# Transposing k and q of six chunks in 64x64 tiles of the TensorE array, one PSUM bank for each chunk

## The chip, the cores and the metric

The kernel runs on one core of one Trainium2 chip. The metric is the device time of one execution in microseconds (us); lower is better. "The span" is the time from the first to the last instruction in the profile of one execution; the device time holds the span and a little around it.

## What is computed

A sliding-window causal attention feeds a gated feed-forward block. Cut to what matters:

```
scores = q @ k.T / sqrt(64)           # 8 batches, 8 heads, 576 positions, head size 64
mask   = 0 <= (query - key) < 64      # each query sees itself and the 63 keys before it
x      = softmax(scores, mask) @ v    # -> [4608 tokens, 512]
out    = (silu(x @ w_gate) * (x @ w_val)) @ w_out     # 512 -> 1536 -> 512
```

Inputs and the output are float32 in memory; on the chip nearly all operands are bfloat16, with sums in float32 in PSUM.

## The kernel before

The 4608 tokens are cut into 36 chunks of 128 tokens for the attention, and into 9 tiles of 512 tokens (four chunks) for the feed-forward block. One list of operations is written out by hand in the function build (L1020). A small planner (class _Graph) keeps the order in which the operations stand in that list for each engine, and puts in a semaphore wait wherever an operation reads what another engine wrote, or overwrites what another engine still reads. So every engine works strictly through its own list, and an operation that has to wait holds up all that stand behind it on its engine.

**The attention of a chunk** needs kT and qT, that is k and q with the head dimension along the partitions. Loads bring k and q in with tokens along the partitions. There are three ways to turn them round:
- Chunks 0 to 3 go through first_T and first_ev (L816, L833) at the start.
- Chunks 10 to 35 go through the function T (L360), a transposing DMA on SyncE's queue.
- Chunks 4 to 9 are turned by TensorE, a pair of chunks (256 tokens) at a time. These three pairs are what the change touches. Pair 4/5 and pair 8/9 go through T2 (L371, TensorE work at L382). Pair 6/7 goes through first_T(..., 1) (L816, TensorE work at L825) and first_ev (L833), because its loads lie in another layout.

In T2 a partition of the source holds two neighbouring tokens, so 128 partitions hold the 256 tokens of the pair. For one of k and q it issues 16 transposes. Each takes 128 partitions x 64 columns (one head, one of the two tokens) as the loaded operand, streams a 128x128 identity past it, and writes 64 partitions x 128 columns of PSUM. The two heads of a couple (index p) go to the lower and the upper 64 PSUM partitions, so two such transposes stand side by side in the array. All 16 fill one PSUM bank with both chunks of the pair. ScalarE (called ACT in the profile) then copies the bank to kT or qT, as one copy of 128x1024 elements, or as two of 128x512 where the ring of chunk slots wraps (q of pair 8/9) or in first_ev (one for each chunk). All copies are made at L260. k and q are separate operations in separate banks.

**The scores** of two chunks are made by S2 (L735): for each chunk Sb (L450) issues 24 small matmuls on 64x64 tiles (L464 and L468), and ACT takes the exponential (L476, two operations for each chunk). The scores of a chunk need kT of the chunk before and of itself, and its own qT. **The weighted sum over v** follows in AV2 (L741, TensorE work at L582), which issues 64 matmuls of 64x64 tiles for two chunks; later pairs go through B2 and AVpair (L692).

**The feed-forward block** F(c, (f,)) (L896) makes 128 of the 1536 hidden columns for 512 tokens: four matmuls with Wg (L888), a tanh on ACT (L869), four matmuls with Wv (L888), and two operations on VectorE (DVE; L874, L876). O (L910) is the second matrix product (12 matmuls at L930), with its copy out and its store. X (L762) turns a finished attention chunk round for the feed-forward block: four TensorE transposes (L784) and a copy (L260).

**PSUM banks.** There are eight. The function bank (L225) gives the bank that was last touched by the oldest operation in the list, except those in the set held; pair (L235) gives two neighbouring banks, and two (L492) two banks that both stay in held until they are taken out.

The order around the three pairs, as it stands in build:

```
F(0,(6,))  T2(2,"k") T2(2,"q")            F(0,(7,))  S2(4)  F(0,(8,)) F(0,(9,)) AV2(4) F(0,(10,))
first_T k, first_T q, first_ev k6, k7     X(4)  F(0,(11,)) with X(5) inside  first_ev q6, q7  F(1,(0,1),0,256)  S2(6) ...
F(1,(5,))  T2(4,"k") T2(4,"q")            F(1,(6,))  S2(8)  F(1,(7,)) ...
```

The loads are issued by GpSimd (POOL): those of pair 4/5 in early_loads (L984, load2 at L332), those of pair 6/7 in more_loads (L992, next_load at L803), followed there by Wo (load_wo, L347), and those of pair 8/9 in late_loads (L1000).

Of the kernel before, what the change touches and what calls it, by code (L numbers as in the profile page):

```python
# [7 lines left out]
B, H, S, D = 8, 8, 576, 64  # L8
DM, DFF = H * D, 1536
T = B * S  # L10
# [7 lines left out]
BF = dt.bfloat16  # L18
# [135 lines left out]
class _Kernel:  # L154
# [213 lines left out]
        self.g.op("sp", lambda e: e.dma_start_transpose(d, src[:, :]), reads=[(x + "n", i, j) for j in range(2)],  # L368
                  writes=[(x + "T", z, 0), (x + "T", z, 1)], dma=True)

    def T2(self, st, x):  # L371
        src = (self.ks2 if x == "k" else self.qs2)[st % 2]
        dst = self.kT if x == "k" else self.qT
        nz = self.NZ if x == "k" else self.ZQ
        bank, bk = self.bank("a")
        tb = bank.bitcast(BF).rearrange("p (c j t) -> p c j t", c=4, j=2)

        def pe(e):
            for c in range(4):
                for j in range(2):  # L380
                    for p in range(2):
                        r = e.transpose(tb[64 * p:64 * p + 64, c, j, :], src[:, 2 * c + p, j, :], self.ident[:, :])  # L382
            return r

        self.g.op("pe", pe, reads=["ident", ("s2", x, st % 2, 0), ("s2", x, st % 2, 1)], writes=[bk])
        a = tb.rearrange("p c j t -> p c t j")

        def ev(eng, lo=0, hi=2):
            z0 = (2 * st + lo) % nz
            if z0 + hi - lo > nz:  # L390
                ev(eng, 0, 1)
                ev(eng, 1, 2)
                return
            d = dst[:, :, 128 * z0:128 * (z0 + hi - lo)].rearrange("p c (t j) -> p c t j", j=2)
            self.copy(eng, d, a[:, :, 64 * lo:64 * hi, :], [bk], [(x + "T", z, b) for z in range(z0, z0 + hi - lo) for b in range(2)])

        return ev

    def var(self, n):
        b0 = (2 * n) % BPB == 0  # L400
        b1 = (2 * n + 1) % BPB == 0
        return 1 if b0 else (2 if b1 else 0)
# [359 lines left out]
    def X(self, n, eng="sp", kind="f"):  # L762
        if n >= NCH:
            return
        g = self.g
        ix, it, u = n % 4, (n // 4) % self.NX, n % 4
        xb = self.xb[ix]
        xo = self.xT[it][:, :, 128 * u:128 * u + 128]
        xk = [("xb", ix, 0), ("xb", ix, 1)]
        if eng == "sp":  # L770
            g.op("sp", lambda e: e.dma_start_transpose(xo, xb[:, :]), reads=xk, writes=[("xT", it, u)], dma=True)
            return
        self.Xp(n, kind)(eng)
# [122 lines left out]
    def F(self, c, fs, lo=0, hi=512, mid=None, side=False):  # L896
        do = self.Fp(c, fs, lo, hi, side)
        for a in range(len(fs)):
            do("Wg", a)
        if mid:  # L900
            mid()
        do("tan", 0)
        for a in range(len(fs)):
            do("Wv", a)
        do("end", 0)
# [112 lines left out]
        self.T(n, "q")  # L1018

    def build(self):  # L1020
        F, S, AV, X, T2, O = self.F, self.S, self.AV, self.X, self.T2, self.O
        self.loads()
        self.banks("a", [4, 5, 6, 7, 0, 1, 2, 3, 4, 5, 0, 1, 2, 3, 4, 5, 6, 7, 0, 1, 2, 3, 4, 5, 6, 7, 6, 7])
        self.lru = True
# [3 lines left out]
        fk = self.first_T("k")  # L1028
        self.first_ev("k", 0, "dve", fk)
        fq = self.first_T("q")  # L1030
# [6 lines left out]
        fk = self.first_T("k", 1)  # L1037
# [3 lines left out]
        s2 = self.Sa(2, True)  # L1041
        fq = self.first_T("q", 1)
# [40 lines left out]
        F(0, (4,))  # L1083
        F(0, (5,))
        F(0, (6,))
        T2(2, "k")("act")
        T2(2, "q")("act")
        self.late_loads()
        F(0, (7,))
        self.S2(4)  # L1090
# [1 line left out]
        F(0, (9,), side=True)  # L1092
        self.AV2(4)
        F(0, (10,))
        fk = self.first_T("k", 1)
        self.held.add(fk[1][1])
        fq = self.first_T("q", 1)
        self.held.add(fq[1][1])
        self.first_ev("k", 6, "act", fk)
        self.first_ev("k", 7, "act", fk)  # L1100
        self.held.discard(fk[1][1])
        X(4, "act")
        F(0, (11,), mid=lambda: X(5, "act"))
        self.first_ev("q", 6, "act", fq)
        self.first_ev("q", 7, "act", fq)
        self.held.discard(fq[1][1])
        F(1, (0, 1), 0, 256)
        self.S2(6)
        F(1, (2, 3), 0, 256)
# [10 lines left out]
        F(1, (4,))  # L1120
        self.init_kmask()
        F(1, (5,))
        T2(4, "k")("act")
        T2(4, "q")("act")
        for n in (10, 11):
            self.load(n, "v", self.lastF)
        for n in (12, 13):
# [31 lines left out]
        for c in range(2, NFC):  # L1159
            for u in range(4):  # L1160
                n = 4 * c + u + 4
# [6 lines left out]
                v = u + 1 if c == 2 else u  # L1168
# [71 lines left out]
```

## Time and profile before

| what | value |
|---|---|
| device time, median of 3 runs | 326.89 us (326.6 to 327.25) |
| span of the profiled execution | 324.8 us |
| that execution's own device time | not listed apart from the runs; the median is 2.1 us above the span |
| mean granted TensorE clock | 1.000 |
| VectorE busy | 215.8 us (66%) |
| ACT busy | 125.8 us (39%) |
| GpSimd busy | 104.2 us (32%) |

The page of the profile lists busy times, a strip of 40 slices, the chain of work that ended last, and groups of instructions with the same line and shape. "PE" is TensorE's matmuls and "PEld" its operand loads, which run beside them. Views of the trace used below: the chain in order of time (start, length, what), the timeline (start, length, engine, line, operation, tiles, count, and in brackets the idle time before it with what ended it), groups by line and shape (count, busy us, mean ns of one, idle time), windows (start:end, length, then busy time and number of instructions that touch the window, granted clock, DMA share, GB/s), the list of waits (us in total, times, longest) and DMA issues (count, KB each, us from issue to landing). Times in these views count from the start of the span. A matmul's listed length holds its way through the array; the next one starts long before it ends, so TensorE's pace is read from starts.

### The profile page before, as it was taken

The numbers are of one execution on the slowest core, as the hardware profiler recorded it, in microseconds if no ns is written. First come the engines' busy times: TensorE is split into PE (matmuls) and PEld (weight loads), VectorE is DVE, ScalarE is ACT, GpSimd is POOL, SyncE is SP. The second block draws the span as 40 slices with busy tenths as digits, with TensorE's granted clock in tenths as the row PEclk, the third lists the DMA queues.
The fourth block names the chain that finished last, engine by engine and source line by source line (L and its number), as shares of the span: only waits on it lengthen the run. The fifth ranks groups of instructions, "written<-read, shape, count | busy, mean of one in ns | idle before, by whom it ended". The sixth has DMA issues, their size and how long they took to land.

```text
span 324.8 us, 7717 instructions
## 1 busy us (share of the span) xinstructions
PE 319.2 (98%) x3278; PEld 162.4 (50%) x3278; DVE 215.8 (66%) x400; ACT 125.8 (39%) x224; POOL 104.2 (32%) x134
## 2 busy tenths in 40 slices
PE   6999999999999999999999999999999999999996
PEld 5665565564544454545454444545454544444444
DVE  5886866688485966676768585958576767555510
ACT  3935563634332443333333242424242422222311
POOL 6999831142626061607060607060402000000000
DMA  7999999999999899959998998999687202000012
GB/s 189 179 191 186 205 172 167 161 150 149 158 138 167 128 100 137 163 109 152 119 115 122 146 141 81 146 132 163 71 110 96 69 32 67 32 34 32 32 67 97
DMA packets 154354, 39.83 MB, mean 123 GB/s; under 512 B 140368, under 2 KB 149328, under 8 KB 154320
## 3 DMA queue, kind: packets, MB, share of 16 engines
q0 software_dynamic: 104896, 18.36, 72.8%
q1 hardware_dynamic: 43952, 11.15, 24.7%
q10 hardware_dynamic: 5472, 9.83, 9.5%
q8 instruction: 26, 0.43, 0.5%
q14 instruction: 8, 0.07, 0.1%
HBM read 37.75 MB, written 9.44 MB: 145 GB/s over the span
## 4 chain that ended last, share of the span: by engine, by line
PE 96%; DMA 1%; ACT 1%; DVE 0%; SPq 0%; issue 0%
PE ps L888 58%; PE ps L930 29%; PE ps L692 2%; PE ps L514 2%; DMA hT<-in_q_dram 1%; PE ps L464 1%; PE ps L825 1%; ACT pt L447 1%; PE ps L382 1%; PE ps L420 1%; PE ps L582 1%; PE ps L468 0%; DVE ost L261 0%; PE ps L784 0%; PE ps L439 0%; ACT xT L260 0%
## 5 line engine op out<-in xcount | busy, mean ns | idle before, releaser
L874 DVE SCALAR_TENSOR_TENSOR uu<-sig,ps 128x512 bf16<-128x512 bf16 x108 | 73.9, 685 | 57.3 <-ACT sig L869 57.1
L888 PE MATMUL ps<-xT,Wg 128*128 128x512 bf16 (+1 forms) x456 | 111.2, 369 | 0.1
L888 PE MATMUL ps<-xT,Wv 128*128 128x512 bf16 (+1 forms) x456 | 111.0, 368 | 0.0
L869 ACT ACTIVATE sig<-ps 128x512 bf16<-128x512 f32 x108 | 65.1, 603 | 89.0 <-PE ps L888 89.0
L930 PE MATMUL ps<-Wo,hT 128*128 128x512 bf16 (+1 forms) x444 | 98.8, 374 | 0.0
L876 DVE SCALAR_TENSOR_TENSOR hT<-uu,ps 128x512 bf16<-128x512 bf16 x108 | 74.2, 687 | 3.7
L888 PEld LDWEIGHTS ps<-xT,Wv 128*128 128x128 bf16 x456 | 44.5, 98 | 48.4
L930 PEld LDWEIGHTS ps<-Wo,hT 128*128 128x128 bf16 x444 | 43.3, 98 | 49.2
L888 PEld LDWEIGHTS ps<-xT,Wg 128*128 128x128 bf16 x456 | 42.7, 98 | 45.5 <-ACT xT L260 0.6
L330 POOL DMA_DIRECT2D kn<-in_k_dram x29 | 24.9, 861 | 107.7 <-PE ps L888 103.7
L330 POOL DMA_DIRECT2D va<-in_v_dram x40 | 34.4, 889 | 34.0 <-PE ps L888 34.0
L260 ACT ACTIVATE ost<-ps 128x512 f32<-128x512 f32 (+1 forms) x22 | 12.9, 587 | 52.9 <-PE ps L930 52.9
L261 DVE COPY ost<-ps 128x512 f32<-128x512 f32 (+1 forms) x15 | 10.1, 674 | 30.1 <-PE ps L930 30.1
L524 ACT ACTIVATE pt<-ps 128x512 bf16<-128x512 f32 x36 | 18.6, 603 | 29.0 <-PE ps L514 29.0
L330 POOL DMA_DIRECT2D qn<-in_q_dram x29 | 25.1, 870 | 0.3 <-issue 0.3
L476 ACT ACTIVATE pt<-ps 128x512 bf16<-128x512 f32 x28 | 14.5, 603 | 12.9 <-PE ps L468 12.9
L727 DVE TENSOR_TENSOR xb<-ps,rc 128x512 bf16<-128x512 f32 (+2 forms) x39 | 18.8, 510 | 0.5
L692 PE MATMUL ps<-va,pt 64*64 64x65 bf16 x800 | 12.3, 192 | 0.0
L490 DVE TENSOR_TENSOR pt<-pt,kmask 128x1024 bf16<-128x1024 bf16 x18 | 11.5, 683 | 0.0
L692 PEld LDWEIGHTS ps<-va,pt 64*64 64x64 bf16 x800 | 10.3, 107 | 0.0
L723 DVE RECIPROCAL rc<-ps 128x8 f32<-128x8 f32 (+2 forms) x39 | 5.7, 174 | 6.5 <-PE ps L692 6.5
L490 DVE TENSOR_TENSOR pt<-pt,mask 128x1024 bf16<-128x1024 bf16 x14 | 9.3, 686 | 0.9 <-ACT pt L476 0.8
(76 smaller groups left out, 131.6 us busy)
## 6 DMA issues: line engine op xcount, KB each, us to landing
out_dram<-ost ACTq DMA_DIRECT2D x35, 256.0 KB, 2.9
va<-in_v_dram POOLq DMA_DIRECT2D x32, 128.0 KB, 5.5
kn<-in_k_dram POOLq DMA_DIRECT2D x23, 128.0 KB, 4.2
qn<-in_q_dram POOLq DMA_DIRECT2D x23, 128.0 KB, 4.5
Wg<-in_moe_w_gate_dram POOLq DMA_DIRECT2D x6, 256.0 KB, 6.6
Wv<-in_moe_w_val_dram POOLq DMA_DIRECT2D x6, 256.0 KB, 7.4
Wo<-in_moe_w_out_dram POOLq DMA_DIRECT2D x2, 768.0 KB, 15.3
ks<-in_k_dram POOLq DMA_DIRECT2D x2, 256.0 KB, 7.1
```

What stands on the lines that cost most here:

```text
L260: return self.g.op("act", lambda e: e.activation(d, a, ACTF.Copy), reads=reads, writes=writes, after=after)
L330: self.g.op("pool", lambda e, d=d, a=a: e.dma_start(d, a), writes=ks, dma=True, after=gate)
L476: g.op("act", lambda e, po=po, p=p: e.activation(po, sv[p], ACTF.Exp, scale=SCALE), reads=[bx[p][1]], writes=[pk[p]])
L490: self.g.op("dve", lambda e: e.tensor_tensor(pt, pt, m, ALU.mult), reads=pk + mk, writes=pk)
L524: g.op("act", lambda e, po=po, p=p: e.activation(po, sv[p], ACTF.Exp, scale=SCALE), reads=[bx[p][1]], writes=[pk[p]])
L692: x = e.matmul(o, ab[0], ab[1], start=first, stop=phase == 1, skip_group_check=True)
L727: g.op("dve", lambda e, av=av, hs=hs, w=w, rc=rc, xo=xo: e.tensor_tensor(xo[:, :, hs, :], av[:, :, :, 0:64], rc[:, :, hs].unsqueeze(3).to_ ...
L869: g.op("act", lambda e: e.activation(sig[:, 0:w], G[:, 0:w], ACTF.Tanh, scale=0.5), reads=[gk], writes=[("sig", i)])
L874: g.op("dve", lambda e: e.scalar_tensor_tensor(uu[:, 0:w], sig[:, 0:w], 1.0, G[:, 0:w], ALU.add, ALU.mult), reads=[("sig", i), gk], writes ...
L876: g.op("dve", lambda e: e.scalar_tensor_tensor(out, v3(uu), 0.5, v3(V), ALU.mult, ALU.mult), reads=[("uu", i), vk], writes=[("hT", ih, f) ...
L888: r = e.matmul(bank[:, a * n:a * n + n], W[:, kk, f * 128:f * 128 + 128], xT[:, kk, lo:hi], start=(kk == 0), stop=(kk == NK - 1))
L930: r = e.matmul(OB[:, 0:n], hT[:, f, 128 * u:128 * u + 128], self.Wo[:, f, lo:hi], start=(f == 0), stop=(f == NF - 1))
```

## The change

T2 goes, and one function T64 turns k and q of a pair in one TensorE operation. Each transpose now takes 64 partitions x 64 columns as the loaded operand, streams 64 columns of the identity, and writes 64 partitions x 64 columns. The index u (chunk of the pair, partitions 64u to 64u+63 of the source) picks the PSUM bank, and p the half of the PSUM partitions. A bank then holds k (first half) and q (second half) of one chunk. There are 64 transposes for a pair where there were 32 (16 for k, 16 for q). The two banks are taken by two(), each held until both copies of its chunk stand in the list. The copies are four for each pair, 128x512 each: in Tkq2 (pairs 4/5 and 8/9) in the order k, q of the first chunk, k, q of the second; for pair 6/7 the first chunk's two before X(4) and the second's two after F(0,(11,)), where k of both chunks stood before and q of both after. For pairs 4/5 and 8/9 a copy now reads PSUM in a row and writes every second element of kT or qT; before, it read PSUM with a step and wrote in a row. Loads, scores and everything else stay as they are.

```diff
-    def T2(self, st, x):
...
-            for c in range(4):
-                for j in range(2):
-                    for p in range(2):
-                        r = e.transpose(tb[64 * p:64 * p + 64, c, j, :], src[:, 2 * c + p, j, :], self.ident[:, :])
...
+    def T64(self, st):
+        n = 2 * st
+        bx = self.two()
+        loads = []
...
         def pe(e):
+            for i, (x, src, _) in enumerate(loads):
+                for a in range(8):
+                    for u in range(2):
+                        r = slice(64 * u, 64 * u + 64)
+                        for p in range(2):
+                            o = bx[u][0].bitcast(BF)[64 * p:64 * p + 64, 512 * i + 64 * a:512 * i + 64 * a + 64]
+                            y = src[r, a, p, :] if st == 3 else src[r, 2 * (a // 2) + p, a % 2, :]
+                            z = e.transpose(o, y, self.ident[r, r])
+            return z
+
+        rd = ["ident"] + [k for _, _, ks in loads for k in ks]
+        self.g.op("pe", pe, reads=rd, writes=[b[1] for b in bx])
+
+        def ev(x, u, eng):
+            bank, bk = bx[u]
...
+            if st == 3:
+                a, d = a.rearrange("p (j g c) -> p c g j", j=8, c=4), d.rearrange("p c (g j) -> p c g j", j=8)
+            else:
+                a, d = a.rearrange("p (c j t) -> p c j t", c=4, j=2), d.rearrange("p c (t j) -> p c j t", j=2)
+            self.copy(eng, d, a, [bk], [(x + "T", z, 0), (x + "T", z, 1)])
+            left.discard((x, u))
+            if not any(v == u for _, v in left):
+                self.held.discard(bk[1])
...
+    def Tkq2(self, st):
+        ev = self.T64(st)
+        for u in range(2):
+            for x in "kq":
+                ev(x, u, "act")
...
-        T2(2, "k")("act")
-        T2(2, "q")("act")
+        self.Tkq2(2)
...
-        fk = self.first_T("k", 1)
-        self.held.add(fk[1][1])
-        fq = self.first_T("q", 1)
-        self.held.add(fq[1][1])
-        self.first_ev("k", 6, "act", fk)
-        self.first_ev("k", 7, "act", fk)
-        self.held.discard(fk[1][1])
+        ev = self.T64(3)
+        ev("k", 0, "act")
+        ev("q", 0, "act")
         X(4, "act")
         F(0, (11,), mid=lambda: X(5, "act"))
-        self.first_ev("q", 6, "act", fq)
-        self.first_ev("q", 7, "act", fq)
-        self.held.discard(fq[1][1])
+        ev("k", 1, "act")
+        ev("q", 1, "act")
...
-        T2(4, "k")("act")
-        T2(4, "q")("act")
+        self.Tkq2(4)
```

More of the change, by code (lines that the diff above doesn't have):

```diff
@@ L369, in T @@
                   writes=[(x + "T", z, 0), (x + "T", z, 1)], dma=True)
-    def T2(self, st, x):
[L372 to L376, printed above, removed]
-        def pe(e):
-            for c in range(4):
-                for j in range(2):
-                    for p in range(2):
[L382 to L395, printed above, removed]
-        return ev
@@ new lines, in T64 @@
+    def T64(self, st):
[4 more added lines that the diff above has]
+            if st == 3:
+                loads.append((x, *self.first[x, 1]))
+            else:
+                loads.append((x, (self.ks2 if x == "k" else self.qs2)[st % 2], [("s2", x, st % 2, i) for i in range(2)]))
+        def pe(e):
+            for i, (x, src, _) in enumerate(loads):
[11 more added lines that the diff above has]
+            bank, bk = bx[u]
+            i = "kq".index(x)
+            a = bank.bitcast(BF)[:, 512 * i:512 * i + 512]
+            z = (n + u) % (self.NZ if x == "k" else self.ZQ)
+            d = (self.kT if x == "k" else self.qT)[:, :, 128 * z:128 * z + 128]
+            if st == 3:
+                a, d = a.rearrange("p (j g c) -> p c g j", j=8, c=4), d.rearrange("p c (g j) -> p c g j", j=8)
+            else:
+                a, d = a.rearrange("p (c j t) -> p c t j", c=4, j=2), d.rearrange("p c (t j) -> p c t j", j=2)
+            self.copy(eng, d, a, [bk], [(x + "T", z, 0), (x + "T", z, 1)])
+            left.discard((x, u))
+            if not any(v == u for _, v in left):
+                self.held.discard(bk[1])
+        left = {(x, u) for x in "kq" for u in range(2)}
+        return ev
@@ L399, in var @@
+    def Tkq2(self, st):
+        ev = self.T64(st)
+        for u in range(2):
+            for x in "kq":
+                ev(x, u, "act")
     def var(self, n):
@@ L1020, in build @@
     def build(self):
-        F, S, AV, X, T2, O = self.F, self.S, self.AV, self.X, self.T2, self.O
+        F, S, AV, X, O = self.F, self.S, self.AV, self.X, self.O
         self.loads()
```

## The prediction

> **What bounds the kernel now.** I read the page first: how busy each engine is, and which chain ended last.
>
> ```profile
> span 324.8 us, 7717 instructions
> PE 319.2 (98%) x3278; PEld 162.4 (50%) x3278; DVE 215.8 (66%) x400; ACT 125.8 (39%) x224; POOL 104.2 (32%) x134
> PE 96%; DMA 1%; ACT 1%; DVE 0%; SPq 0%; issue 0%
> ```
>
> TensorE is busy for 98% of the span and makes up 96% of the chain. So time taken off TensorE shortens the run, unless a wait appears where it was. Next the chain in order of time: the three pairs stand on it as TensorE work.
>
> ```profile
> 28.16 1.01 PE ps L382 x32
> ...
> 37.83 1.01 PE ps L825 x32
> ...
> 55.46 1.01 PE ps L382 x32
> ```
>
> That is all that can be won: 3 x 1.01 = 3.0 us, 0.9% of the span. Third, the list of waits: who already waits around these places?
>
> ```profile
> PEld ps L464 <- ACT qT L260: 0.8, 2, 0.4
> ...
> PEld ps L888 <- ACT xT L260: 0.6, 2, 0.3
> ```
>
> Two things on TensorE behind the transposes list ACT copies as what released them: scores (L464) and feed-forward blocks (L888). These are operand loads that could not run ahead; the matmuls' own starts are hardly late. But both are close, and if TensorE comes sooner they can become waits.
>
> **TensorE's part.** Windows show the old transposes from their first start to the next feed-forward matmul, and 64x64 work of the same width elsewhere (AV2, L582).
>
> ```profile
> 28.09:29.11 1.02, 1.02 (x34) 1.00 1.46 198
> ```
> ```profile
> 35.12:35.39 0.27, 0.27 (x33) 1.00 1.14 190
> 35.81:35.93 0.12, 0.12 (x20) 1.00 1.10 179
> ```
>
> The old 32 transposes take 1.02 us with the way out. In AV2 32 tiles of 64x64 start within 0.27 us (the 33rd in the row is a feed-forward matmul still on its way), four abreast, 0.034 us for each four. They stream 65 columns, the new transposes 64, each with its own operand load as AV2's have. AV2's last start to the next feed-forward matmul is 0.12 us. So 64 new ones: 0.27 + 0.26 + 0.12 = 0.65 us, 0.37 less. The way in, a gap between a feed-forward matmul and a tiled one, is there before and after. The trace shows no transpose in 64x64 tiles, so I bound it: below by AV2's pace, 0.65; above by the old transposes, which run only two abreast (64 in twos of half the width are the 1.02 again), and beyond that by no overlap at all (a rival, below). I take AV2's pace: same tile shape, same order of the four tiles, row halves in different banks in both.
>
> **ACT's part, pairs 4/5 and 8/9.** The copies change in number. Here are their prices, then the timeline around pair 4/5.
>
> ```profile
> L260 ACT ACTIVATE qT<-ps 128x512 bf16<-128x512 bf16 x7 | 3.9, 601 | 1.6 <-PE ps L827 1.6
> L260 ACT ACTIVATE kT<-ps 128x1024 bf16<-128x1024 bf16 x2 | 2.0, 1023 | 1.7 <-PE ps L382 1.7
> ```
> ```profile
> 28.56 0.61 PE L382 MATMUL ps<-ident,qs 128*64 128x128 bf16 x16
> 28.77 1.02 ACT L260 ACTIVATE kT<-ps 128x1024 bf16<-128x1024 bf16 x1 [0.84 <-PE ps L382]
> 29.69 1.02 ACT L260 ACTIVATE qT<-ps 128x1024 bf16<-128x1024 bf16 x1
> 30.59 0.60 ACT L869 ACTIVATE sig<-ps 128x512 bf16<-128x512 f32 x1
> 30.94 0.24 PE L464 MATMUL ps<-qT,kT 64*64 64x128 bf16 x2
> 31.19 0.22 PE L464 MATMUL ps<-qT,kT 64*64 64x128 bf16 x1
> 31.43 2.06 ACT L476 ACTIVATE pt<-ps 128x512 bf16<-128x512 f32 x4 [0.23 <-PE ps L468]
> ```
>
> Before: k's copy starts at 28.77, about 0.25 us after k's last transpose (the first of q starts at 28.56), while q's transposes still run. Both copies are done by 30.71; the scores of chunk 4 start at 30.94 and those of chunk 5 at 31.19. After: all 64 transposes are one operation, so ACT starts 0.25 after the last of them, then does four copies, one each 0.49 us (four exponentials take 2.06: three steps and a last 0.60).
>
> Counted from the first transpose (28.09): last transpose 0.53; copies start at 0.78, 1.27, 1.76, 2.25; the last ends at 2.85. TensorE reaches chunk 4's scores at 30.94 - 28.09 - 0.37 = 2.48; they need the first two copies, done at 1.87: no wait. It reaches chunk 5's scores 0.25 later, at 2.73; they need all four, done at 2.85, and 0.05 us for TensorE to notice (the 40.30 row below ends at 40.90, the load it releases starts at 40.95). So chunk 5 starts at 2.90: **a new wait of 0.17 us**, and 0.37 becomes 0.20. Queued behind that wait is all the rest of TensorE's list. On ACT the tanh of F(0,(7,)) stands behind the four copies: it starts at 28.09 + 0.78 + 4 x 0.49 = 30.83 instead of 30.59, so DVE's two operations on that block and the banks that they free come 0.24 later; the exponentials behind it start at 31.32 instead of 31.43, a little sooner. I cost the later tanh at nothing: the feed-forward blocks after the scores hide it, and where they don't it falls under a rival.
>
> Pair 8/9 has the same shape:
>
> ```profile
> 55.39 0.64 PE L382 MATMUL ps<-ident,ks 128*64 128x128 bf16 x16
> ...
> 58.24 0.24 PE L464 MATMUL ps<-qT,kT 64*64 64x128 bf16 x2
> ...
> 58.49 0.22 PE L464 MATMUL ps<-qT,kT 64*64 64x128 bf16 x1
> ```
>
> 58.24 - 55.39 = 2.85, and 0.25 to the next chunk, as for 4/5: 0.20 again. That the old code needed three copies there (q wrapped) changes nothing in the new sum.
>
> The copies read PSUM in a row now and write every second bfloat16. No ACT row here has such a write. Bounds: below, 0.49 a step (the 512-element copies that read with a step cost 601 ns like the float32 ones that read in a row; a stepped read costs nothing seen); above, twice the element time, 0.49 + 0.42 (1023 less 601 for 512 elements). I take 0.49, nearest in count and type, and make the other a rival. [...]
>
> **Pair 6/7.** Here the second half's copies are moved behind F(0,(11,)), as q's were, so what matters is what stands between.
>
> ```profile
> 37.76 0.64 PE L825 MATMUL ps<-ident,ks 128*64 128x128 bf16 x16
> 38.44 1.09 ACT L260 ACTIVATE kT<-ps 128x512 bf16<-128x512 bf16 x2 [0.84 <-PE ps L825]
> 39.41 0.60 ACT L260 ACTIVATE xT<-ps 128x512 bf16<-128x512 bf16 x1
> 40.30 0.60 ACT L260 ACTIVATE xT<-ps 128x512 bf16<-128x512 bf16 x1 [0.28 <-PE ps L784]
> 40.95 0.77 PEld L888 LDWEIGHTS ps<-xT,Wg 128*128 128x128 bf16 x8 [0.32 <-ACT xT L260]
> 40.96 1.04 PE L888 MATMUL ps<-xT,Wg 128*128 128x256 bf16 x8
> ```
>
> F(1,(0,1)) at 40.96 needs X(5)'s copy, which ended at 40.90. After: ACT does k, q, X(4), X(5) from 0.78 on: 0.78 + 3 x 0.49 + 0.60 + 0.05 = 2.90. TensorE is there at 40.96 - 37.76 - 0.37 = 2.83. A wait of 0.07: the pair keeps 0.30. The moved copies of chunk 7 end at about 41.8, before its scores.
>
> **What else could be late.** T64 waits for k and q both, and for both banks. The tightest load is q of pair 6/7; the next is Wo for O(0,0).
>
> ```profile
> 25.89 0.71 POOL L808 DMA_DIRECT2D qs<-in_q_dram  x1
> ```
> ```profile
> qs<-in_q_dram POOLq DMA_DIRECT2D x1, 256.0 KB, 11.0
> ```
> ```profile
> 44.43 0.68 POOL L330 DMA_DIRECT2D kn<-in_k_dram  x1 [3.06 <-DMA Wo<-in_moe_w_out_dram]
> ```
> ```profile
> 45.19 0.60 PE L930 MATMUL ps<-Wo,hT 128*128 128x512 bf16 x2
> ```
>
> q lands at 36.9; T64 comes at 37.76 - 0.20 = 37.56: 0.66 us to spare, where k's transposes used not to wait for q at all. Wo has landed by 44.43; O comes at 45.19 - 0.20 - 0.30 = 44.69: 0.26 to spare. Banks: pair 4/5 takes two, pair 6/7 two, pair 8/9 two, in the same turn of the eight as before, since each bank's last touch keeps its place in the list.
>
> **Sum.** 0.20 + 0.30 + 0.20 = 0.70 us off the profiled execution's 324.8. The device time is that span plus what lies around it (the median of 326.89 is 2.1 above), which the change does not touch: 326.89 - 0.70 = **326.2 us**. A measurement of this kernel can tell about 0.2%, 0.65 us, from no change; so the forecast sits just beyond that line.
>
> **The rivals.**
> - *The waits do not come*, because the copies follow closer or TensorE's pieces between are longer than I read: three times 0.37, 325.8 us. For: the waits are 0.17 and 0.07 out of chains of 2.9. Against: rows that agree within 0.02. Chance 0.17.
> - *Given back.* Part of the 0.70 is lost at a place with little to spare (Wo 0.26, q of 6/7 0.66, or DVE's work behind the later tanh), or AV2's pace is not quite met: 0.2 to 0.6 remains, 326.3 to 326.7 us. Chance 0.13.
> - *Only column halves overlap*: row halves take turns, 1.02 us as before. The copies then start up to 0.5 later than k's did, and both kinds of wait stay (0.17, 0.07, 0.17): 327.3 us. For: no transpose here runs in row halves. Against: the scores and AV2 do, four abreast. Chance 0.06.
> - *Slower: the stepped write doubles ACT's element time.* Place: the four copies of pairs 4/5 and 8/9. Steps of 0.91 instead of 0.49 and a last copy of 1.02: the chain grows by 3 x 0.42 + 0.42 = 1.7, all of it a wait of chunk 5's and chunk 9's scores: 2 x 1.7 - 0.70 = 2.7 slower, 329.6 us. It decides from 0.09 us more a copy on (0.70 / 8). Chance 0.09.
> - *Slower: no overlap at all.* The row that shows full-width transposes one by one:
>
> ```profile
> 40.04 0.22 PE ps L784 x4
> ```
>
>   0.055 us for 128 columns, so 0.0275 for 64, times 64 = 1.76, and 0.12 out: 0.86 more than before at each pair, with the waits 3 x 0.86 + 0.41 = 3.0 slower, 329.9 us. Against: the old transposes are twice as quick for their width (1.01 for 32), and AV2 is three times as quick. Chance 0.03. [...]
>
> **How the numbers follow.** Forecast as summed: 0.52, with about 0.15 us either way (326.0 to 326.4), of which some two thirds lies beyond 0.65 us. Faster by over 0.2%: 0.35 + 0.17 = 0.52. Within 0.2%: 0.17 + 0.13 + 0.06 = 0.36. Slower: 0.09 + 0.03 = 0.12. The range runs from the first rival with a little scatter of the runs (325.5) to the row-halves case (327.3); what lies above is 0.12.
>
> **What would show it.** Right: windows from the transposes' start to the next feed-forward matmul of about 0.65 instead of 1.02 at all three pairs; four kT and qT copies of about 600 ns for each pair; TensorE loads of chunk 5's and chunk 9's scores that wait about 0.2 us for ACT qT; the span about 0.7 shorter. Wrong: copies of 900 ns or more (the stepped write); transposes that start in twos (row halves); TensorE waiting for a qs load or Wo; the three windows short but the end no earlier, which would mean a later wait that this profile does not show.

## The result and the profile after

The changed kernel takes 328.66 us (median of 11 runs, 327.22 to 329.72); the kernel before, beside it, 326.47 us (11 runs, 325.81 to 328.18). The ratio is 1.006, 95% interval 1.0042 to 1.0078: slower by 0.4 to 0.8%, where 326.2 us had been forecast, in a range from 325.5 to 327.3. The profiled execution of the changed kernel took 327.78 us with a span of 325.9 us; it is the fifth quickest of the eleven.

The lines that answer to those of before lie 20 further on in the code: feed-forward matmuls are L908, output matmuls O L950, scores L484 and L488, the attention-value matmuls of a single chunk L712, the transposes L389. (The edits of e1, e3 and e7 to e9 move them 10 further still, that of e10 28; L898 in e2 and e4 is L888 of before.) From the page:

```profile
span 325.9 us, 7911 instructions
PE 319.0 (98%) x3374; PEld 161.9 (50%) x3374; DVE 215.6 (66%) x400; ACT 125.8 (39%) x227; POOL 104.1 (32%) x134
```

TensorE is busy for 0.2 us less, with 96 matmuls and 96 operand loads more. The span is 1.1 us longer all the same. The forecast's first two signs come as expected. Windows of the changed kernel, from the first transpose of each pair to the next other work of TensorE:

```profile
28.00:28.64 0.64, 0.64 (x66) 0.60 (x65) 0.61 (x2) 0.00 (x0) 0.64 (x1) 1.00 1.46 197
37.46:38.10 0.64, 0.64 (x65) 0.60 (x65) 0.61 (x3) 0.00 (x0) 0.64 (x2) 1.00 1.25 210
54.79:55.43 0.64, 0.64 (x65) 0.60 (x65) 0.63 (x2) 0.00 (x0) 0.05 (x1) 1.00 1.62 156
```

Sixty-four transposes take 0.64 us (0.65 forecast). The eight copies that write every second element stand in these two rows with seven others (minimum, median, maximum in ns), and none of them takes more than 653:

```profile
L260 ACT ACTIVATE qT<-ps x9: 591/597/653, 7.4 to 57.0; 128x512 bf16<-128x512 bf16 x9
L260 ACT ACTIVATE kT<-ps x6: 597/600/641, 28.8 to 56.5; 128x512 bf16<-128x512 bf16 x6
```

The third sign is not in the list of waits, but the starts show it: the second chunk's scores wait for the last copy, as summed. Timeline around pair 4/5, then around pair 8/9:

```profile
30.22 0.62 ACT L260 ACTIVATE qT<-ps 128x512 bf16<-128x512 bf16 x1
...
30.47 0.24 PE L484 MATMUL ps<-qT,kT 64*64 64x128 bf16 x2
...
30.89 0.24 PE L484 MATMUL ps<-qT,kT 64*64 64x128 bf16 x2
```
```profile
57.01 0.62 ACT L260 ACTIVATE qT<-ps 128x512 bf16<-128x512 bf16 x1
...
57.26 0.24 PE L484 MATMUL ps<-qT,kT 64*64 64x128 bf16 x2
...
57.68 0.24 PE L484 MATMUL ps<-qT,kT 64*64 64x128 bf16 x2
```

The copy ends at 30.84 and chunk 5 starts at 30.89, 0.42 behind chunk 4 where it was 0.25: a wait of 0.17. Chunk 9 starts 0.42 behind chunk 8 in the same way. Up to here the forecast holds: TensorE reaches O(0,0) at 44.64 instead of 45.19, and chunk 9's scores at 57.68 instead of 58.49, 0.81 ahead. Of that, 0.09 was there before the first transpose (28.00 against 28.09), so the change has won 0.72 by then, where the sum says 0.70. Then, behind the last pair, the chain shows what the profile of before had nowhere:

```profile
57.71 0.20 PE ps L484
57.90 0.00 PE ps L488
57.91 0.62 issue
58.52 0.22 PE ps L488 x2
```

In the list of waits the two largest on TensorE, behind one at the start of the kernel:

```profile
PE ps L712 <- issue: 0.8, 1, 0.8
PE ps L488 <- issue: 0.6, 1, 0.6
```

And the timeline around the second:

```profile
64.16 0.23 PE L712 MATMUL ps<-va,pt 64*64 64x65 bf16 x3
65.21 0.38 PE L712 MATMUL ps<-va,pt 64*64 64x65 bf16 x22 [0.82 <-issue]
```

TensorE stops twice in the middle of one operation, among 64x64 matmuls whose operands are all there, and nothing that the profile shows releases it ("issue"). From start to start the gaps are 0.83 us (57.69 to 58.52) and 1.02 us (64.19 to 65.21). The feed-forward and output matmuls that follow start later by that: the O block that began at 78.89 before begins at 79.91.

So the books for this execution close to within 0.06. TensorE was 0.81 ahead in front of the first stop and is 1.02 behind at that O block, so 1.83 was lost, and the two gaps less the usual spacing (some 0.04 each) are 1.77.

What are these stops? Windows from one resumption to the next, and as many instructions back again from the first (busy us and number of instructions on PE, then on PEld):

```profile
58.50:65.18 6.68, 5.86 (x126) 3.16 (x125) 4.25 (x7) 3.48 (x8) 0.00 (x0) 1.00 2.14 166
50.12:58.50 8.38, 7.81 (x128) 3.87 (x127) 3.88 (x9) 5.32 (x11) 1.77 (x2) 1.00 1.66 152
```

251 and 255 matmuls and loads, 256 each time with TensorE's semaphore instructions, which the view leaves out: the two stops lie 256 TensorE instructions apart, and 256 before the first the count leads to 50.1 us. The view of DMA queues has a queue "instruction" (q8) with 26 packets and 0.43 MB in the whole span, about 16 KB each. The packets that fall ahead of the stops, in windows 56.2 to 57.3 and 63.0 to 64.1 (queue, packets, MB, share):

```profile
q8 instruction: 1, 0.02, 5.3%
```
```profile
q8 instruction: 1, 0.02, 5.5%
```

None follows between 57.3 and 58.5, nor between 64.1 and 65.2. That gives the theory for the experiments, **instruction blocks**. TensorE's list is counted off in blocks of 256 instructions, so that both stops fall between two blocks; such a place is a limit, a block is entered when TensorE crosses the limit ahead of it, and a packet of this queue is called a fetch. That TensorE needs the packet before it can enter the next block is the author's assumption; no view shows what a packet holds or what sets it off. What the trace shows: in the four blocks entered from 35.9 us on, the packet ends 5.3, 5.0, 7.1 and 5.5 us later (at 41.15, 47.53, 57.21 and 64.01), and the two stops end 1.3 and 1.2 us after the last two packets (at 58.52 and 65.20). A block of mostly feed-forward matmuls lasts longer than that (13.5 us from the limit at 92.8 to that at 106.3). A block with many 64x64 matmuls need not: the 256 instructions from 58.52 on were used up in 5.7 us. The change adds 192 instructions, and so both fills blocks with short work and shifts every later block limit.

Rival theories: the stops come with 64x64 transposes as such (their number, or what they leave behind); or the stops are an accident and the gain is lost to operand waits.

### The profile page after: what moved, and what is told of

Same layout as the page of the kernel before. It is cut to its first block, busy times and chain, and to the rows that moved or that the text cites. A ratio compares the mean times of both kernels' runs of the same rounds, so it can differ in the third digit from the quotient of the medians.

```text
span 325.9 us, 7911 instructions
## 1 busy us (share of the span) xinstructions
PE 319.0 (98%) x3374; PEld 161.9 (50%) x3374; DVE 215.6 (66%) x400; ACT 125.8 (39%) x227; POOL 104.1 (32%) x134
## 4 chain that ended last, share of the span: by engine, by line
PE 94%; DMA 2%; POOL 2%; DVE 1%; issue 1%
PE ps L908 58%; PE ps L950 29%; PE ps L712 2%; DMA Wv<-in_moe_w_val_dram 2%; PE ps L534 2%; PE ps L484 1%; POOL va L330 1%; PE ps L389 1%; PE ps L488 1%; PE ps L602 0%; PE ps L804 0%; POOL ks L828 0%; PE ps L565 0%; POOL qs L828 0%; POOL Wg L345 0%
## 5 line engine op out<-in xcount | busy, mean ns | idle before, releaser
L894 DVE SCALAR_TENSOR_TENSOR uu<-sig,ps 128x512 bf16<-128x512 bf16 x108 | 73.8, 683 | 57.6 <-ACT sig L889 57.2
L908 PE MATMUL ps<-xT,Wv 128*128 128x512 bf16 (+1 forms) x456 | 110.9, 368 | 0.5 <-DMA Wv<-in_moe_w_val_dram 0.5
L908 PE MATMUL ps<-xT,Wg 128*128 128x512 bf16 (+1 forms) x456 | 111.1, 368 | 0.0
L889 ACT ACTIVATE sig<-ps 128x512 bf16<-128x512 f32 x108 | 65.2, 604 | 90.3 <-PE ps L908 90.3
L950 PE MATMUL ps<-Wo,hT 128*128 128x512 bf16 (+1 forms) x444 | 98.8, 373 | 0.0
L908 PEld LDWEIGHTS ps<-xT,Wv 128*128 128x128 bf16 x456 | 44.5, 98 | 49.1 <-DMA Wv<-in_moe_w_val_dram 0.6
L950 PEld LDWEIGHTS ps<-Wo,hT 128*128 128x128 bf16 x444 | 43.3, 98 | 49.2
L908 PEld LDWEIGHTS ps<-xT,Wg 128*128 128x128 bf16 x456 | 42.7, 98 | 45.3 <-ACT xT L260 0.4
L712 PE MATMUL ps<-va,pt 64*64 64x65 bf16 x800 | 12.5, 192 | 0.8 <-issue 0.8
L712 PEld LDWEIGHTS ps<-va,pt 64*64 64x64 bf16 x800 | 10.4, 107 | 0.9 <-issue 0.9
(76 smaller groups left out, 132.5 us busy)
```

The lines of the kernel that those rows point to most:

```text
L712: x = e.matmul(o, ab[0], ab[1], start=first, stop=phase == 1, skip_group_check=True)
L889: g.op("act", lambda e: e.activation(sig[:, 0:w], G[:, 0:w], ACTF.Tanh, scale=0.5), reads=[gk], writes=[("sig", i)])
L894: g.op("dve", lambda e: e.scalar_tensor_tensor(uu[:, 0:w], sig[:, 0:w], 1.0, G[:, 0:w], ALU.add, ALU.mult), reads=[("sig", i), gk], writes ...
L908: r = e.matmul(bank[:, a * n:a * n + n], W[:, kk, f * 128:f * 128 + 128], xT[:, kk, lo:hi], start=(kk == 0), stop=(kk == NK - 1))
L950: r = e.matmul(OB[:, 0:n], hT[:, f, 128 * u:128 * u + 128], self.Wo[:, f, lo:hi], start=(f == 0), stop=(f == NF - 1))
```

## The experiments

Each row is a median in us; the ratio is to the kernel before, run on the same chip (326.20, 326.38 and 326.40 us in the three groups).

| kernel | us (runs) | ratio, 95% | stops of TensorE in the profiled execution, and when each ends |
|---|---|---|---|
| e1 after, 32 matmuls more | 326.19 (12) | 0.9997 (0.9988 to 1.0006) | none |
| e2 before, 96 more | 327.69 (7) | 1.0072 (1.0043 to 1.0101) | 0.91 until 65.26 |
| e3 after, 56 more | 329.93 (4) | 1.0107 (1.0092 to 1.0121) | 0.19 until 13.99, 2.54 until 40.80 |
| e4 before, 56 more | 326.91 (12) | 1.0021 (1.0011 to 1.003) | 0.34 until 13.80, 0.50 until 66.37 |
| e5 after, no DMA transposes of 10, 11 | 326.88 (12) | 1.0007 (0.9992 to 1.0022) | 0.35 until 50.84, 0.13 until 58.71 |
| e6 before, the same left out | 325.94 (12) | 0.9984 (0.9967 to 1.0001) | none |
| e7 e1, half of the copies on DVE | 326.23 (12) | 0.9995 (0.9979 to 1.0011) | none |
| e8 e1, loads in another order | 326.41 (12) | 0.9996 (0.998 to 1.0013) | 0.37 until 15.60, 0.19 until 63.80 |
| e9 e1, no DMA transposes of 10, 11 | 326.01 (11) | 0.9987 (0.9976 to 0.9999) | none |
| e10 after, pair 8/9 in the old form | 326.98 (12) | 1.0022 (1.0005 to 1.004) | 0.26 until 65.03 |

**e1 to e4: move the block limits, and nothing else.** Small matmuls of zeros are put between the k and q transposes at the start of the kernel, into banks that are written anew afterwards; each is two TensorE instructions. e1 has 32 of them on top of the change, e2 has 96 on the kernel before (as many instructions as the change adds, all earlier), e3 and e4 have 56 on either.

```diff
+    def pad(self, count):
+        def pe(e):
+            for i in range(count):
+                u, p = i // 2 % 2, i % 2
+                r = slice(64 * u, 64 * u + 64)
+                x = e.matmul(self.ps[3 * u][64 * p:64 * p + 64, 0:32], self.wz[r, 0:64], self.wz[r, 0:32], start=True, stop=True)
+            return x
+        self.g.op("pe", pe, reads=["wz"])
...
         self.first_ev("k", 0, "dve", fk)
+        self.pad(32)
         fq = self.first_T("q")
```

Expected of e1:

> The changed kernel with 32 tiny matmuls (64 more TensorE instructions, 32 columns of zeros each, written to PSUM banks that nothing reads) in a gap of TensorE near 6.5 us. Theory F: TensorE stops where its instruction stream has run through a block of 256 instructions before the next block has come, so it matters where in the stream the bursts of small matmuls lie. From pair 8/9 on, 64 more instructions put the block limits back where they lie in the kernel before (192 + 64 = 256). F expects the two stops at 57.9 and 64.4 us (0.6 and 0.8) to go, at most 0.5 us to show up near 41, and 325.8 to 326.6 us. Rival W (the changed work or its waits cost the time, wherever the blocks lie): the stops stay, and the time is that of the changed kernel, 328.7, or a little more.

Of e2:

> The kernel before, its transposes untouched, with 96 of the same tiny matmuls (192 instructions, what the change adds) near 6.5 us. F expects stops like those of the changed kernel from about 58 us on, above all one of 0.6 to 1.0 us near 64, and 327.0 to 328.0 us. W expects no stop and the time before, 326.5, plus at most 0.3 for a start held up by the tiny matmuls.

Of e3:

> The changed kernel with 56 tiny matmuls (112 instructions) near 6.5 us. With the block limits so, one block would be used up between 34.9 and 38.2 us, within 3.3 us, while a fetch took about 6.5 us there. F expects one stop of 2 to 3.5 us near 38 us, none at 57.9 and 64.4, and 328 to 329.5 us. W expects the stops where they were and 328.7 to 329.

Of e4:

> The kernel before with 56 tiny matmuls (112 instructions) near 6.5 us. One block would be used up between 63.0 and 66.0 us. F expects one stop of 1.3 to 3 us near 66 us and 327.5 to 329.5 us. W expects no stop and 326.5 to 326.8.

*Measured.* More work made the changed kernel faster: e1, with 32 matmuls more than the kernel after, takes 326.19 us instead of 328.66 (the kernel before beside them: 326.20 and 326.47). And the kernel before, which has none of the new transposes, gets the stop and the loss with 96 idle matmuls (e2, 327.69). Its chain:

```profile
64.29 0.06 PE ps L692 x3
64.35 0.91 issue
65.26 0.44 PE ps L692 x25
```

The line is the same operation as the second stop of the kernel after, at the same place in the list. So 64x64 transposes are not needed for a stop; a block limit in the wrong place is enough. e3 moves the limit into X(4), behind pair 6/7. Its chain:

```profile
37.46 0.64 PE ps L389 x64
38.10 0.16 PE ps L804
38.26 2.54 issue
40.80 0.46 PE ps L804 x3
41.26 1.71 PE ps L918 x4
```

One stop, near 38 as expected, of 2.54 us; the time (329.93) lies a little above the 328 to 329.5 expected. The rest of it is in the last row, four feed-forward matmuls in 1.71 us where four take 0.86 elsewhere. Windows of e3, with the granted clock third from the end:

```profile
38.20:40.80 2.60, 0.06 (x1) 0.00 (x0) 1.34 (x3) 1.05 (x2) 1.63 (x2) 1.00 1.25 208
40.80:41.40 0.60, 0.60 (x4) 0.41 (x4) 0.00 (x0) 0.10 (x1) 0.36 (x1) 0.54 1.23 205
41.40:44.10 2.70, 2.70 (x11) 1.21 (x10) 0.00 (x0) 1.16 (x3) 0.33 (x1) 0.50 1.69 184
44.10:47.00 2.90, 2.90 (x67) 2.23 (x65) 2.06 (x3) 2.08 (x5) 1.99 (x3) 0.97 2.43 157
```

After the long stop the clock is granted at half for some 3.4 us (an estimate from the 0.54, 0.50 and 0.97 of these windows), and the span is 3.5 us above that of e1 (328.3 against 324.8). Behind the two stops of the kernel after and the one of e2 the windows show 1.00 (58.5 to 60 and 65.2 to 70; 65.2 to 68). The mean granted clock of this execution is 0.995; three of the 35 executions of the kernel before beside e5 to e8 have the same mean and took 328.06 to 328.10 us, so it may meet a long stop at times too, which no trace shows.

e4 stops at 65.88, where it should, but for 0.50 us and not 1.3 to 3, and the time is 326.91 instead of 327.5 or more. The place was right and the size too large. When a fetch arrives isn't fixed: in the traces of the kernels before and after the packet ends anywhere from 3.2 us before the block ahead is entered (before, 287.21 against 290.39) to 7.1 us after (after, 57.21 against 50.14). That is the part that can't be worked out beforehand from a profile of another kernel.

The count places all of the stops. Matmuls and loads from the start of the span up to the stop near 65 us, in the kernel after, e2 and e4:

```profile
0.00:65.20 65.20, 60.99 (x972) 36.39 (x972) 45.64 (x98) 36.20 (x68) 40.99 (x59) 1.00 1.61 180
0.00:65.25 65.25, 62.51 (x972) 37.95 (x972) 45.70 (x98) 36.48 (x66) 41.07 (x59) 1.00 1.60 180
0.00:66.36 66.36, 63.43 (x972) 38.83 (x972) 47.32 (x105) 37.46 (x67) 41.13 (x59) 1.00 1.59 179
```

The same 972 and 972 stand ahead of it in three different lists of work. With TensorE's 40 semaphore instructions and one drain the trace of the kernel after has 1985 TensorE instructions there, 193 more than 7 times 256. Counted in the traces of the kernels before and after, with what each edit adds, every other stop of the kernel after, e3, e4, e5 and e8 comes behind 449, 1217, 1473, 1729 or 1985 (one more or less), each 193 more than a multiple of 256. The count gives 26 such limits in the kernel after, and its queue has 26 packets. Taken in order, the first packet with the second limit, no limit in the traces of the kernels before and after is crossed sooner than 1.2 us after its packet has ended (1.78 in the one, 1.19 in the other).

e1 also says what is left without stops: 326.19 against 326.20, no gain. Timeline and chain of e1:

```profile
44.73 1.02 PE L960 MATMUL ps<-Wo,hT 128*128 128x512 bf16 x4 [0.46 <-issue]
...
55.59 0.45 PE L389 MATMUL ps<-ident,ks 64*64 64x64 bf16 x32 [0.65 <-DMA qs<-in_q_dram]
```
```profile
35.27 20.28 DMA qs<-in_q_dram
```

TensorE, in this execution 0.59 us ahead before the first transpose already (27.50 against 28.09), waits 0.46 us ahead of O(0,0), whose Wo landed at 44.63, and 0.65 us for q of pair 8/9, which landed at 55.55. (In the kernel before that q landed at 52.78; here it lands 2.8 us later, shortly before the DMA transpose of chunk 10's k, which landed at 56.08.) The O block of 78.89 starts at 78.91. In this execution the two loads take back the head start and what the transposes save.

**e5 and e6: is it the DMA transposes that make fetches late?** SP's four DMA transposes of chunks 10 and 11 are left out, in the kernel after (e5) and the kernel before (e6); the scores of these two chunks then read what the buffers hold.

```diff
-        for n in (10, 11):
-            self.Tkq(n)
```

Of e5:

> The changed kernel without the four transposing DMAs of chunks 10 and 11 (k and q), which run from about 47 to 61 us: the part left out is the turning of those two chunks, whose scores are made from what older chunks left in kT and qT. Same TensorE instructions, so the blocks of the stream lie as in the changed kernel. Theory F with busy DMA engines as the reason why a fetch is late (FD): in the changed kernel the fetches from 50 to 64 us came 7.1 and 5.5 us after the block ahead was entered; without the transposes they come within 5, the stops at 57.9 and 64.4 us shrink from 1.4 us together to 0.3 or less, and the time is 325.4 to 326.2 us. Rival FC (a fetch takes 5 to 7 us there whatever the DMA engines do): both stops stay, 328 to 329 us.

Of e6:

> The kernel before with the same four transposing DMAs left out (the same part of the computation is left out). It tells what leaving them out is worth where nothing stops: FD and FC both expect 325.9 to 326.4 us, as before. Against it the kernel of e5 should be 0.3 to 0.8 us faster under FD, 1.5 to 2.5 slower under FC.

*Measured.* Half true. e5 gains 1.8 us on the kernel after, but its 326.88 us lie above the 325.4 to 326.2 expected, 0.9 us above e6 where it should be faster. From 57 us on, where these transposes would run, fetches do come sooner: in e6 the packet falls between 57.2 and 58.3, when the block ahead was entered at 57.1; in the kernel before it fell between 61.0 and 62.1, the block ahead entered at 57.3. The rows, e6 first:

```profile
q8 instruction: 1, 0.02, 6.0%
```
```profile
q8 instruction: 1, 0.02, 5.6%
```

The two stops shrink from 0.6 and 0.8 to 0.13 and none, but another comes, 0.35 until 50.84, among X's transposes:

```profile
PE ps L804 <- issue: 0.4, 1, 0.4
```

And the longest stop of all, e3's of 2.54 us, ends at 40.80, where the kernel after issues its first DMA transpose at 46.75; beside the packet in e3's window from 38.2 to 39.6 only the loads' queue q0 is at work (282 packets, 120.3%). That DMA transposes alone delay the fetch falls. Nor are busy DMA engines enough: e6's quick packet falls in a window in which q0 has 249.9% and q1 40.7%, while in the kernel before, from 57.3 to 61.0, ahead of its late packet, they have 117.6 and 28.3%. What makes one fetch late and another quick stays open.

**e7 and e8: the two loads.** e7 is e1 with the second chunk's copies of pairs 4/5 and 8/9 on DVE; e8 is e1 with pair 8/9's loads ahead of chunk 11's.

```diff
-                ev(x, u, "act")
+                ev(x, u, "dve" if u else "act")
```
```diff
-        for n in (10, 11):
-            self.load(n, "kq")
+        self.load(10, "kq")
         self.load2(4, "k")
         self.load2(4, "q")
+        self.load(11, "kq")
```

Of e7:

> The kernel of e1 with the copies of the second chunk of pairs 4/5 and 8/9 on VectorE, those of the first chunk on ACT. The wait of the second chunk's scores (0.17 us in the prediction) should fall to 0.05 or less at pair 4/5, so that the stretch from the first transpose to the feed-forward block behind the scores falls from 3.27 to about 3.1 us. Whether the end comes sooner is open: in e1 TensorE waited for Wo near 44.7 us and for q of pair 8/9 near 55.6. If loads set the pace there, 326.0 to 326.3 us; if not, 325.7 to 326.0.

Of e8:

> The kernel of e1 with the loads of pair 8/9 issued ahead of those of chunk 11 (they stood behind them). In e1 TensorE waited 0.65 us for q of pair 8/9, which landed at 55.55. If that wait is what eats the gain, q lands near 51 us, the wait goes, and the time is 325.5 to 325.9. Against it: chunk 11's transposing DMAs end some 3 us later, near 64 us, where its scores begin (63.9); if those then wait, 326.2 to 328.

*Measured.* Neither gains in the median. In e7's profiled execution (325.74 us, one of its quicker ones) the new wait of chunk 5 is gone, as expected (3.11 us from the first transpose to the feed-forward matmuls behind the scores, 3.27 in e1), and q came in time but for 0.13; the next wait is Wo:

```profile
44.38 1.46 PE L960 MATMUL ps<-Wo,hT 128*128 128x512 bf16 x6 [0.26 <-issue]
```

In e8's profiled execution (327.6 us, the slowest of its twelve) the wait for q of pair 8/9 is gone, and chunk 11, whose loads now come later, waits in its place:

```profile
PE ps L484 <- DMA qT<-qn: 0.8, 1, 0.8
```

**e9: no stops and no late q.** e1 without the four DMA transposes (as in e5, the scores of chunks 10 and 11 read what the buffers hold).

> The kernel after with the 32 small matmuls of e1, and without the four DMA transposes of chunks 10 and 11 (left out: their scores then read what the buffers hold). If the sum of 0.70 was right and is lost only to stops of the instruction stream and to the two loads seen in e1: no stop over 0.2 us; the load of q of chunks 8 and 9 lands before 53.5 again (52.8 in the kernel before) and its wait of 0.65 goes; the wait for Wo of about 0.4 stays. O(0,0) 0.4 to 0.5 earlier than in e6, the feed-forward matmuls after the transposes of chunks 8 and 9 another 0.2, so span about 323.9 to 324.1 (e6: 324.6) and a time of 325.2 to 325.6, 0.3 to 0.7 below e6. If something else eats the gain: as e6, 325.8 to 326.2, with the pair's 0.37 given back before O(0,48).

*Measured.* In the profiled execution most of it comes. q of pair 8/9 lands at 52.70, no stop, no wait for q. The operand loads of O(0,0) start at 44.27 (e6: 44.96; some of e9's matmul records are missing, so the loads are compared). The wait for Wo that was to stay isn't seen, as Wo landed at 44.21. The O block that begins at 78.70 in e6, as the first row shows, begins at 77.87 here:

```profile
78.70 1.03 PE L930 MATMUL ps<-Wo,hT 128*128 128x512 bf16 x4
```
```profile
77.87 0.38 PE L960 MATMUL ps<-Wo,hT 128*128 128x512 bf16 x1
```

0.83 ahead, of which 0.21 was there before the first transpose (27.76 against 27.97): the change has won 0.62, and the span is 323.8 instead of 324.6. The medians don't show it: 326.01 us, where 325.2 to 325.6 was expected and 325.8 to 326.2 if something else ate the gain, against 325.94 for e6. Both ratios to the kernel before are uncertain by more than 0.1% either way, so a gain of 0.2% is neither shown nor excluded. In the trace most of the forecast's 0.70 is there; whether it reaches the typical execution stays open.

**e10: undo one part.** The transposes of chunks 8 and 9 alone go back to the old form (T2, two copies).

```diff
-        self.Tkq2(4)
+        self.T2(4, "k")("act")
+        self.T2(4, "q")("act")
```

> The kernel after, with the transposes of chunks 8 and 9 put back to the old form, so 32 matmuls (64 instructions) fewer from 55 us on. By the theory of instruction blocks the limits move the other way than in e1: the block entered at 50.1 is as in the kernel after, and the next limit falls at about 60.6 us, with no stop there; the block after it is then used up by 64.6 us, 4 us later, while its fetch took 2.1 to 6 us plus 1.2 to 1.35 here: a stop of 0 to 3 us, likeliest 1 to 2.5, at about 64.6, in the 64x64 matmuls or the feed-forward matmuls behind them. The time: 326.4 - 0.5 + 1 to 2.5, so 326.9 to 328.4. If the stops come from the number of small matmuls, and not from where the limits lie: no stop after 55 us, or one smaller than the two of the kernel after, and 325.9 to 326.2, as the part that is left (0.20 + 0.30) says.

*Measured.* 326.98 us, slower than the kernel before by 0.05 to 0.4%, though it keeps the two pairs that save 0.50 in the sum; the theory that counts small matmuls gave 325.9 to 326.2. The profiled execution (326.54) shows a stop at the place named, now within a feed-forward operation:

```profile
63.94 0.83 PE L936 MATMUL ps<-xT,Wg 128*128 128x256 bf16 x6
65.03 0.39 PE L936 MATMUL ps<-xT,Wg 128*128 128x256 bf16 x2 [0.26 <-issue]
```

0.26 us, within the 0 to 3 that was expected but below the 1 to 2.5 called likeliest. Six of the other executions took 327.4 to 328.4 and were not traced, so a longer stop in those is likely and not shown.

What the ten settle: stops appear, move and vanish with the number of instructions ahead of them, on both kernels, with matmuls of zeros put in (e1 and e3 against after, e2 and e4 against before) or transposes taken out (e10 against after), and they come at one count modulo 256. What they don't: what sets a fetch off, what delays it, and why no block in the two traces is entered sooner than 1.2 us after its packet; these are read from the times and were not varied. The entry into the block ahead can't be all of it: in the kernel after, one packet ends at 129.5 while the limit ahead of it is crossed at 132.5. No version's median here is below the kernel before by more than 0.2%.

## Why the prediction was wrong

- *TensorE's part, 0.37 a pair*: right. 0.64 us instead of 1.02. AV2's pace was the right row, and neither "only column halves overlap" nor "no overlap" happened.
- *The new wait in front of chunk 5's scores, 0.17*: right, 30.89 less 30.47 less the usual 0.25. From the first transpose of pair 4/5 to the feed-forward matmuls behind both scores it took 3.27 us (28.00 to 31.27) instead of 3.48: 0.21, forecast 0.20. Chunk 9 has the same 0.42 between the chunks (57.26 to 57.68), just ahead of the first stop. In e7, with half of the copies on DVE, the wait was gone.
- *Pair 6/7 keeps 0.30*: right, 2.90 (37.46 to 40.36) instead of 3.20.
- *The stepped write costs nothing*: right, medians of 597 and 600 ns, where copies that wrote in a row took 601 and 594 in the mean before. The rival that made the run slower by it (329.6) came near the measured time for a reason that did not exist.
- *What else could be late*: half right. Wo had been given 0.26 to spare, and it is the first wait once TensorE comes earlier still (0.46 in e1 and 0.26 in e7, where TensorE was some 0.6 ahead before the first transpose). q of pair 6/7 was no trouble. q of pair 8/9 was not looked at, and was late in e1 by 0.65.
- *Sum*: this is the step that failed. The 0.70 itself was right (0.72 by chunk 9's scores). But the sum takes it off a span of 324.8 in which everything else on TensorE stays as it was: time saved was to shorten the run "unless a wait appears where it was", and the sum has no term for a stop of TensorE that no operand or bank causes. It put that at nothing without a reason. The change does alter something that has no row of its own in a list of operations: it puts 192 more instructions into TensorE's stream, at first sight free because their time on TensorE was already counted. They moved the limits of its blocks into two stretches of 64x64 matmuls behind the last pair. That cost 1.77 us in the profiled execution. Six of the other ten executions were slower still, by 0.9 to 1.9 us, and weren't traced; the median lost 2.2 us against the kernel before and so some 2.9 against the sum, which the same cause would explain with longer stops, but that is worked out and not seen.
- *The base of the sum* was off as well, the other way: 326.89 was the median of three runs, and eleven give 326.47. In nearly every run listed the device time lies 1.7 to 1.9 us above that run's own span; the 2.1 compared a median with the span of another execution.
- *The rivals*: none named the instruction stream, so the chance of 0.12 for slower rested on two mechanisms that the traces now refute. The last sentence on what would show it wrong ("the three windows short but the end no earlier, which would mean a later wait that this profile does not show") describes what happened, and had no price and no chance.

It could have been bounded. In the trace of before the same fetch packets are there, and the block limit at 63.84 was crossed 1.78 us after its packet had ended, where the two stops of the kernel after end 1.2 and 1.3 us after theirs and e3's an estimated 1.4 (its packet starts at 38.47 and takes 0.9): 0.4 to 0.6 us to spare, of the size of the terms that the prediction did write down. A fetch took 4.8 us there (57.3 to 62.1) and the block lasted 6.6 (57.28 to 63.84). A change that adds 192 instructions ahead of such a place can use its margin up, by where the limits fall. A range that held this would have reached from 325.8 to about 329, an estimate after the fact that puts a stop of 1 to 3 us in place of the gain.

## What to carry to other kernels

When a change alters how many instructions an engine issues, find the packets of the queue "instruction" in the trace first: see where the limits fall (here every 256 TensorE instructions), how long each block lasts against how late its packet came (here up to 7.1 us after the block was entered), and which limits the new count shifts into a stretch of short instructions. Here stops put down to "issue" in the middle of one operation, 256 instructions apart, pointed to that; 32 filler matmuls far ahead, in one run (e1), told it from a cost of the changed work. And before counting on 0.2% on the bounding engine, list the next loads in its path with their landing times, all of them: in e1's profiled execution Wo and q of the last pair took back what the stops had left.

## What had not been expected of the hardware

- TensorE stood still for 0.1 to 2.5 us while everything that the profile lists for it had landed, at one count modulo 256 of its instructions; the stops of the kernel after end 1.2 and 1.3 us after a packet of the queue "instruction". 64 to 192 instructions more or fewer moved the two kernels between 326.2 and 329.9 us.
- After the stop of 2.54 us (e3) the granted clock was half for some 3.4 us (0.50 and 0.54 in the windows), and the span grew by 3.5 us against e1. Behind the stops of 0.83 and 1.02 us (kernel after) and 0.91 (e2) the windows show 1.00.
- 64 transposes of 64x64 take 0.64 us with the way out where 32 of twice the width and twice the rows took 1.02; copies that write every second bfloat16 took 597 to 600 ns in the median, those that wrote in a row 601 and 594 in the mean (kernel before).
